# Fused attention and two feed-forward layers: the first weight conversions start ten steps later, and their raw loads move from the Activation queue to the SyncE queue

## The chip, the cores and the metric

The kernel runs on one NeuronCore of a Trainium2 chip. The metric is device microseconds of one execution, as the median of several runs. The engines are named as the profile names them: PE (TensorE), DVE (VectorE), ACT (ScalarE), POOL (GpSimd) and SP (SyncE, which here only issues DMAs). Before the change the median of three runs is 1136.29 us (1132.78 to 1137.8).

## The reference

Three stages follow one another. An attention whose weights below a threshold are set to zero is followed by a feed-forward layer with a squared ReLU and by a second one with the Mish activation:

```python
# q, k, v: (4 batches, 8 heads, 576 rows, 64)
scores = scale * np.matmul(q, k.transpose(0, 1, 3, 2))
thresh = np.max(scores, axis=-1, keepdims=True) - tau
scores = np.where(scores >= thresh, scores, -1000000000.0)
attn = np.exp(scores - max); attn = attn / (sum + 1e-09)
x = (attn @ v) reshaped to 2304 tokens x 512
# first layer, d_ff = 2048
r = np.maximum(x @ w_in, 0.0);  g = s * (r * r) + b;  x = g @ w_out
# second layer, d_ff = 2048
h = x @ w_in2;  g = h * np.tanh(softplus(h));  out = g @ w_out2
```

## The kernel before

**Attention.** Two heads are one pair, so there are 16 pairs, four for each batch of 576 tokens. Each pair is worked in nine row tiles. For every tile `scores` (L338 to L363) has PE make the score tile S in four matmuls, DVE take the row minimum of the negated scores (ns, L342), ACT the exponential (e, L349), DVE the cut (L353) and POOL the normalisation (L363). `weights_t` (L376 to L387) transposes one chunk on PE into T, which ACT copies to te. `products_v` (L403, L406) multiplies by v into pv in two portions, one after the chunk te_6 and one after te_8; the second ends the pair, and `split_x` (L414, L415) casts pv to xh and xl. Transposed chunks run seven tiles behind the scores. There is one buffer for T, so a transposition waits until ACT has copied the one before it.

**Preparing the next pair.** While a pair is scored, `prep_qk` (L294) transposes the next pair's k and then q, ACT casts the transposed tile to its high part (hik and hiq, L278), DVE subtracts to get the low part (lok and loq, L279), and six (k) or four (q) DMAs of 144 KB move halves of these tiles to the partitions where the score matmuls read them (L299, "moves"). The tiles hi and lo have one buffer each, so hiq can only be written when the moves that read hik have landed. All these DMAs are issued on SP, in order. `self.moved` holds the last move that was issued.

**The first layer's weights.** Its weights arrive as 64-bit floats and are converted in 32 units of 512 KB, by `split_w` (L47). For one unit a DMA loads the raw words (wraw, L59), ACT rescales them (L65), DVE puts the single-precision number together in three operations (wa, L67 to L69), ACT casts it to the high part (wp, L72), and DVE (POOL in the first four pairs) subtracts to get the low part (L73). The unit is then stored to DRAM for later batches (L194, on SP). `split_all` runs units as a pipeline: each call of `next(w1)` loads one more unit and takes every unit under way one step further, so a unit is finished by the fifth call after its load. There are four buffers for the raw words and five (`ring`) for finished units.

**The order of the work.** The first four pairs are issued by a loop of their own in `run` (L804 to L808), since the feed-forward layer needs all four pairs of a batch. In that loop `next(w1)` is called at every tenth step from step 42 on. After it the first layer of batch 0 (`moe1`) and the further attention are woven together by a table of costs, and `first` (L814) calls `next(w1)` once for every unit of the layer. The program's instructions are not executed as they are written: a scheduler of the compiler sets the order on each engine, and it moves conversions ahead of where they are written. `keep_in_program_order` and `issue_after` limit it. In that order each engine works strictly one instruction after another, and a DMA that has to wait for its semaphore or its buffer holds up whatever stands behind it on the engine that issues it.

Of the kernel before, what the change touches and what calls it, by code (L numbers as in the profile page):

```python
# [19 lines left out]
class Fused:  # L20
# [26 lines left out]
    def split_w(self, src, hi, lo, pool, tags, kw):  # L47

        nc = self.nc
        i = self.nd
        self.nd += 1
        n = src.shape[1] * src.shape[2] // 2
        raw = pool.tile([P, n, 2], I32, tag=tags[0], name=f"wraw{i}", **kw)
        self.tc.keep_in_program_order(nc.scalar.dma_start(raw.rearrange("p (c f) w -> p c (f w)", c=src.shape[1]), src))  # L59
        low, high = raw[:, :, 0], raw[:, :, 1]  # L60
        hf = high.bitcast(F32)
        yield
        yield
        a = pool.tile([P, n], I32, tag=tags[1], name=f"wa{i}")
        self.tc.keep_in_program_order(nc.scalar.activation(hf, hf, AF.Copy, scale=2.0 ** -112))  # L65
        yield
        nc.vector.tensor_scalar(a, high, 3, None, op0=ALU.logical_shift_left)  # L67
        nc.vector.scalar_tensor_tensor(a, low, 29, a, op0=ALU.logical_shift_right, op1=ALU.bitwise_or)
        nc.vector.scalar_tensor_tensor(a, high, -0x80000000, a, op0=ALU.bitwise_and, op1=ALU.bitwise_or)  # L69
        yield  # L70
        af = a.bitcast(F32).rearrange("p (c f) -> p c f", c=src.shape[1])
        nc.scalar.copy(hi, af)  # L72
        (nc.gpsimd if self.s2p else nc.vector).tensor_tensor(lo, af, hi.bitcast(F32), op=ALU.subtract)  # L73
# [295 lines left out]
    def weights_t(self, pr, ci, run):  # L369
        nc = self.nc  # L370
        T = self.tp.tile([P, 1024], F32, tag="T", name=f"T{pr}_{ci}")
        E4 = self.sets[pr % 2][3]
        o = ci * 128
        for i in range(4):
            with self.tc.issue_after(run) if run and i == 0 else nullcontext():
                nc.tensor.transpose(T[:, i * 128:i * 128 + 128], self.es[pr, i, "pair"][:, o:o + 128], self.ident)  # L376
        if ci != 4:
            h = 0 if ci < 4 else 1

            c0 = 64 + o - 576 * h  # L380
            nc.tensor.transpose(T[:, 512:640], E4[:, c0:c0 + 128], (self.ident, self.swap)[h])  # L381
        else:

            nc.tensor.matmul(T[:, 512:576], E4[:, 0:128], self.ident[:, HALVES[1]], start=True, stop=False)
            nc.tensor.matmul(T[:, 512:576], E4[:, 576:704], self.ident[:, HALVES[0]], start=False, stop=True)
        te = self.at.tile([P, 576], F32, tag="te", name=f"te{pr}_{ci}", bufs=7)
        nc.scalar.copy(te, T[:, :576])  # L387
        return te
# [30 lines left out]
    def attention(self):  # L419
# [18 lines left out]
        for k in range(N + LAG + 2):  # L438
# [33 lines left out]
            if 0 <= j < N:  # L472
                prj, ci = divmod(j, 9)
                todo = prj, ci, self.weights_t(prj, ci, run)
                yield 550
# [299 lines left out]
    def run(self, ctx):  # L775
# [27 lines left out]
        k = 0  # L803
        while 3 not in self.x:  # L804
            next(att)
            k += 1
            if k >= 42 and k % 10 == 2:
                next(w1)  # L808

        pro.close()  # L810
# [33 lines left out]
        while a_on or m_on:  # L844
            if a_on and (not m_on or (a_done - 5000.0) / a_left <= m_done / m_left):
                with tc.high_priority(offset=200):
                    c = next(att, None)
                a_on = c is not None
                a_done += c or 0
            else:  # L850
                c = next(mo, None)
# [11 lines left out]
        nc = tc.nc  # L863
# [73 lines left out]
```

## Time and profile before

| | us |
|---|---|
| median of three runs | 1136.29 (1132.78 to 1137.8) |
| the profiled execution | 1133.57 |
| its span, first to last instruction | 1131.8 |
| PE busy in the span | 1081.1 (96%) |
| DVE busy | 806.3 (71%) |
| ACT busy | 619.0 (55%) |
| POOL busy | 263.4 (23%) |
| PE time in the chain that ended last | 67% of the span |

The median of the runs is 2.7 us above the profiled execution. PE is the engine that is busy nearly all the time; its busy time is that of pipelined matmuls and so does not say that it works at its peak. [...]

### The profile page before, as it was taken

How to read it: one execution, taken by the hardware profiler on the slowest of the kernel's cores; microseconds unless marked ns; L12 is line 12 of the kernel's file. 1: busy time of each engine (PE TensorE's matmuls, PEld its weight loads, DVE VectorE, ACT ScalarE, POOL GpSimd, SP SyncE). 2: the span in 40 equal slices, each digit the busy share in tenths (PEclk: the TensorE clock that was granted, in tenths of full speed). 3: DMA queues.
4: the chain of work that ended last, by engine and by line, in shares of the span. 5: the costliest groups of instructions: out<-in, count | busy, mean ns of one | idle time of the engine just before them, and what ended most of it. 6: DMA issues, size and time to landing. Idle time of an engine off the chain costs nothing.

```text
span 1131.8 us, 21384 instructions
## 1 busy us (share of the span) xinstructions
PE 1081.1 (96%) x7964; PEld 1018.7 (90%) x7964; DVE 806.3 (71%) x1746; ACT 619.0 (55%) x1153; POOL 263.4 (23%) x306
## 2 busy tenths in 40 slices
PE   7887799999999999999999989999999999999998
PEld 6765599898999998888989879999999999999998
DVE  6987799999666677878866666735696368725782
ACT  4655497684576665667747557634363244513351
POOL 4533273351352442325334301100000000000000
PEclk9998899999999999999999999999999999999999
DMA  7366585966847869689864599977998999996683
GB/s 163 80 169 167 172 256 207 300 199 203 246 135 215 249 222 278 214 292 302 310 211 141 190 355 365 361 268 282 351 383 319 343 420 367 348 336 253 263 294 117
DMA packets 141591, 292.70 MB, mean 259 GB/s; under 512 B 52848, under 2 KB 78960, under 8 KB 133168
## 3 DMA queue, kind: packets, MB, share of 16 engines
q1 hardware_dynamic: 123408, 274.26, 70.8%
q10 hardware_dynamic: 18080, 17.07, 5.2%
q8 instruction: 63, 1.03, 0.4%
q14 instruction: 40, 0.33, 0.1%
HBM read 201.85 MB, written 66.58 MB: 237 GB/s over the span
## 4 chain that ended last, share of the span: by engine, by line
PE 67%; DVE 3%; DMA 3%; ACT 2%; issue 1%; POOL 0%; DVEq 0%; ACTq 0%; POOLq 0%
PE o L748 16%; PE y L503 13%; PE h L503 12%; PE qY L614 6%; PE qX L614 4%; PE qV L614 4%; PE S L338 3%; PE pv L406 3%; PE T L376 3%; DMA wso<-chlo 1%; DMA wi<-wsi 1%; PE pv L403 1%; PE T L381 1%; DMA w<-w 1%; ACT e L349 0%
## 5 line engine op out<-in xcount | busy, mean ns | idle before, releaser
L363 POOL TENSOR_SCALAR e<-e,st 128x576 f32<-128x576 f32 x128 | 133.4, 1055 | 229.0 <-DVE st L358 163.9
L748 PE MATMUL o<-wo,hl 128*128 128x256 f32 x1512 | 177.7, 279 | 0.0
L748 PEld LDWEIGHTS o<-wo,hl 128*128 128x128 f32 x1512 | 177.4, 188 | 0.0
L503 PE MATMUL y<-gh,w 128*128 128x288 f32 x768 | 165.0, 300 | 3.4 <-ACT y L548 1.7
L503 PE MATMUL h<-xh,w 128*128 128x288 f32 x768 | 164.7, 299 | 1.6 <-ACT xh L414 0.7
L342 DVE TENSOR_SCALAR_CACHE_REDUCE ns<-S 128x576 f32<-128x576 f32 x144 | 108.0, 752 | 53.6 <-PE S L338 53.2
L349 ACT ACTIVATE e<-ns,st 128x576 f32<-128x576 f32 x128 | 99.1, 776 | 64.4 <-DVE ns L342 62.0
L387 ACT COPY te<-T 128x576 f32<-128x576 f32 x144 | 91.8, 637 | 72.4 <-PE T L381 61.7
L353 DVE SCALAR_TENSOR_TENSOR e<-ns,st,e 128x576 f32<-128x576 f32 x128 | 114.9, 899 | 22.6 <-ACT e L349 21.6
L503 PEld LDWEIGHTS y<-gh,w 128*128 128x128 f32 x768 | 126.7, 189 | 4.5 <-ACT y L548 2.0
L503 PEld LDWEIGHTS h<-xh,w 128*128 128x128 f32 x768 | 125.8, 188 | 2.9 <-ACT xh L414 1.2
L527 POOL TENSOR_TENSOR gl<-rr,gh 128x288 fp32r<-128x288 f32 x96 | 93.6, 989 | 128.8 <-ACT rr L526 128.8
L503 PE MATMUL y<-gl,w 128*128 128x288 f32 x384 | 113.9, 297 | 0.9 <-POOL gl L527 0.9
L503 PE MATMUL h<-xl,w 128*128 128x288 f32 x384 | 113.5, 296 | 0.0
L338 PE MATMUL S<-KH,Q 128*128 128x288 f32 x320 | 97.2, 320 | 11.2 <-DVE lok L279 4.1
L376 PE MATMUL T<-ident,e 128*128 128x128 f32 x576 | 92.5, 283 | 15.3 <-ACT te L387 14.7
L376 PEld LDWEIGHTS T<-ident,e 128*128 128x128 f32 x576 | 68.7, 144 | 33.0 <-issue 18.0
L338 PE MATMUL S<-KL,Q 128*128 128x288 f32 x320 | 91.6, 302 | 0.0
L614 PE MATMUL qY<-yc,wi 128*128 128x384 f32 x432 | 86.6, 337 | 1.3 <-DVE g L637 1.3
L406 PE MATMUL pv<-te,rawv 128*64 128x288 f32 x576 | 86.6, 416 | 0.0
L614 PEld LDWEIGHTS qY<-yc,wi 128*128 128x128 f32 x432 | 75.6, 188 | 1.9 <-DVE g L637 1.9
L338 PEld LDWEIGHTS S<-KH,Q 128*128 128x128 f32 x320 | 62.3, 195 | 16.0 <-DVE ns L342 6.6
(150 smaller groups left out, 2204.4 us busy)
## 6 DMA issues: line engine op xcount, KB each, us to landing
w<-w SPq DMA_DIRECT2D x96, 512.0 KB, 5.1
wo<-wso SPq DMA_DIRECT2D x42, 1024.0 KB, 7.0
wi<-wsi SPq DMA_DIRECT2D x23, 1024.0 KB, 7.8
wi<-wsi SPq DMA_DIRECT2D x25, 768.0 KB, 7.4
w<-wp SPq DMA_DIRECT2D x32, 512.0 KB, 4.8
wsi<-chli SPq DMA_DIRECT2D x24, 512.0 KB, 5.1
wso<-chlo SPq DMA_DIRECT2D x24, 512.0 KB, 7.1
ycd<-yp SPq DMA_DIRECT2D x14, 768.0 KB, 8.1
```

What stands on the lines that cost most here:

```text
L338: self.scored = nc.tensor.matmul(so, Q[:, c0:c0 + 128], kt[:, ks], start=(i == 0), stop=(i == len(terms) - 1)).ins
L342: nc.vector.tensor_scalar(ns.rearrange("p (h n) -> p h n", h=2), sv, -0.125, 3.0e38, op0=ALU.mult, op1=ALU.min, accum_out=nm[:, c1])
L349: nc.scalar.activation(e, ns, AF.Exp, bias=nm[:, c1], scale=-1.0)
L353: nc.vector.scalar_tensor_tensor(e, ns, nthr[:, c1], e, op0=ALU.is_le, op1=ALU.mult, accum_out=sm[:, c1])
L363: nc.gpsimd.tensor_scalar(t, t, rinv[:, j:j + 1], u[:, j:j + 1], op0=ALU.mult, op1=ALU.add)
L376: nc.tensor.transpose(T[:, i * 128:i * 128 + 128], self.es[pr, i, "pair"][:, o:o + 128], self.ident)
L387: nc.scalar.copy(te, T[:, :576])
L406: ins = self.nc.tensor.matmul(*args, **kw).ins
L503: nc.tensor.matmul(acc[:, :n], w[:, wl, c], rhs[c][xl][:, ts], start=(i == 0), stop=(i == 11))
L527: (nc.vector if b == 3 else nc.gpsimd).tensor_tensor(gl[:, ts], r2, gh[:, ts].bitcast(F32), op=ALU.subtract)
L614: self.nc.tensor.matmul(acc, a, b, start=(first and i == 0), stop=(i == n - 1), skip_group_check=True)
L748: nc.tensor.matmul(bank[p][t], hl[:, gl, j, ts], w[:, 2 * (q % 2) + j, wl], start=(old is None and q + j + k == 0), stop=(q + j + k == 6), ...
```

## The change

In the loop over the first four pairs the conversion is called from step 52 on and not from 42, which makes five calls of six. In the same stretch (`self.s2p` is set) the raw loads are issued on SP and must stand behind the last of the moves issued so far; afterwards they are issued on ACT as before.

```diff
         raw = pool.tile([P, n, 2], I32, tag=tags[0], name=f"wraw{i}", **kw)
-        self.tc.keep_in_program_order(nc.scalar.dma_start(raw.rearrange("p (c f) w -> p c (f w)", c=src.shape[1]), src))
+        dst = raw.rearrange("p (c f) w -> p c (f w)", c=src.shape[1])
+        if self.s2p:
+            with self.tc.issue_after(self.moved):
+                nc.sync.dma_start(dst, src)
+        else:
+            self.tc.keep_in_program_order(nc.scalar.dma_start(dst, src))
...
             k += 1
-            if k >= 42 and k % 10 == 2:
+            if k >= 52 and k % 10 == 2:
                 next(w1)
```

Five lines are added ahead of L65, so a line of the kernel before is found five lines further down in the changed one.

On SP, around the moves of the fourth pair's q (Q) and the fifth pair's k (KH, KL; the preparation runs ahead of the scores, and these ahead of the products), the order before was this; no raw load stands there:

```order
L299 DMA Q_125<-hiq_807 64x576
L299 DMA Q_125<-loq_808 64x576
L250 DMA rawk<-in_k_dram 128x8x64
L251 DMA rawk<-in_k_dram 64x2x64
L299 DMA KH_119<-hik_1005 64x576 x2
```

In the changed kernel two raw loads stand behind the moves of q and ahead of the next load of k:

```order
L304 DMA Q_125<-hiq_804 64x576
L304 DMA Q_125<-loq_805 64x576
L62 DMA wraw_876<-in_moe_w_in_dram 128x4x256
L62 DMA wraw_989<-in_moe_w_in_dram 128x4x256
L255 DMA rawk<-in_k_dram 128x8x64
L256 DMA rawk<-in_k_dram 64x2x64
L304 DMA KH_119<-hik_1000 64x576 x2
```

The next two raw loads stand likewise behind the q moves of the following pair and ahead of a load of k. The fifth stands behind those of the pair after that, and there two stores (w) come between the moves of its high and its low part:

```order
L304 DMA Q_125<-hiq_1331 64x576 x2
L199 DMA w_0_0_1_1588<-wp_0_1_988 128x1024
L199 DMA w_0_0_2_1681<-wp_0_2_1117 128x1024
L304 DMA Q_125<-loq_1332 64x576 x2
L62 DMA wraw_1373<-in_moe_w_in_dram 128x4x256
```

In the kernel before, these two stores stood ahead of the load of q, and the raw loads were not on SP.

On ACT, the first raw load before stood among the copies te of the second pair; the next two and the first rescaling stood around the cast hik of the fifth pair, which comes while the second pair's products end:

```order
L387 COPY te_8_876<-T_8_870 128x576 [waits PE_49]
L59 DMA wraw_879<-in_moe_w_in_dram 128x4x256 [waits DMAHW4_49]
L349 ACTIVATE e_1_964<-ns_1_961,st_929 128x576 [waits DVE_49,Pool_49]
L278 CAST hik_1005<-tpk_996 128x640 [waits DMAHW2_49,DMAHW0_49,PE_49]
L349 ACTIVATE e_2_983<-ns_2_980,st_929 128x576 [waits DVE_49,Pool_49]
L65 ACTIVATE wraw_763<-wraw_763 128x512 [waits DMAHW6_49]
L59 DMA wraw_994<-in_moe_w_in_dram 128x4x256 [waits DMAHW7_49]
L414 CAST xh_899<-pv_839 128x576 [waits PE_49]
```

In the changed kernel no instruction of the conversion stands there:

```order
L392 COPY te_8_873<-T_8_867 128x576 [waits PE_49]
L283 CAST hik_1000<-tpk_991 128x640 [waits DMAHW7_49,DMAHW1_49,PE_49]
L354 ACTIVATE e_2_980<-ns_2_977,st_926 128x576 [waits DVE_49,Pool_49]
L419 CAST xh_896<-pv_836 128x576 [waits PE_49]
```

At the end of the fourth pair the order of ACT before, from the last conversion to the copy te_6 and the exponentials behind it:

```order
L72 CAST wp_1_0_1234<-wa_1605 128x512 [waits DVE_49]
L65 ACTIVATE wraw_1607<-wraw_1607 128x512 [waits DMAHW4_49]
L59 DMA wraw_1791<-in_moe_w_out_dram 128x4x256 [waits DMAHW1_49,Activation_49]
L387 COPY te_5_1318<-T_5_1312 128x576 [waits PE_49]
L349 ACTIVATE e_0_1205<-ns_5_1364,st_1196 128x576 [waits DVE_49]
L387 COPY te_6_1357<-T_6_1351 128x576 [waits PE_49]
L349 ACTIVATE e_1_1231<-ns_6_1413,st_1196 128x576 [waits DVE_49]
L349 ACTIVATE e_2_1262<-ns_7_1431,st_1196 128x576 [waits DVE_49]
```

In the changed kernel a cast, three rescalings and three raw loads stand between te_6 and te_7:

```order
L392 COPY te_6_1345<-T_6_1339 128x576 [waits PE_49]
L70 ACTIVATE wraw_1373<-wraw_1373 128x512 [waits DMAHW4_49]
L64 DMA wraw_1688<-in_moe_w_out_dram 128x4x256 [waits DMAHW7_49,Activation_49]
L354 ACTIVATE e_2_1250<-ns_7_1419,st_1188 128x576 [waits DVE_49]
L70 ACTIVATE wraw_1595<-wraw_1595 128x512 [waits DMAHW5_49]
L64 DMA wraw_1779<-in_moe_w_out_dram 128x4x256 [waits DMAHW0_49,Activation_49]
L77 CAST wp_1_0_1363<-wa_1686 128x512 [waits DVE_49]
L70 ACTIVATE wraw_1688<-wraw_1688 128x512 [waits DMAHW7_49]
L64 DMA wraw_1851<-in_moe_w_out_dram 128x4x256 [waits DMAHW1_49,Activation_49]
L392 COPY te_7_1394<-T_7_1388 128x576 [waits PE_49]
L354 ACTIVATE e_3_1297<-ns_8_1453,st_1188 128x576 [waits DVE_49]
L392 COPY te_8_1412<-T_8_1406 128x576 [waits PE_49]
```

When the feed-forward layer starts, both kernels have put the same number of these operations behind them on ACT: five casts wp and seven rescalings stand ahead of the layer's first ReLU in either.

## Rows read from the trace of the kernel before

**Rows 1.** Page, the span in 40 slices: busy tenths of PE.
```profile
PE   7887799999999999999999989999999999999998
```
**Rows 2.** Stretches: us, then busy PE, PEld, DVE, ACT, POOL, PEclk, DMA share, GB/s.
```profile
52.96:79.32 26.36, 21.69 (x154) 17.60 (x155) 21.08 (x63) 15.66 (x25) 12.30 (x13) 0.94 0.56 134
79.32:110.75 31.43, 23.42 (x160) 18.96 (x159) 25.44 (x70) 16.99 (x28) 11.28 (x11) 0.89 0.70 175
110.75:140.17 29.42, 22.26 (x134) 16.37 (x133) 21.42 (x60) 14.57 (x24) 6.54 (x5) 0.83 0.64 187
140.17:171.00 30.83, 30.74 (x238) 28.51 (x239) 29.04 (x59) 28.02 (x64) 21.76 (x20) 1.00 0.85 247
```
**Rows 3.** Timeline of ACT, first of the casts xh: start, us, operation.
```profile
52.96 0.64 ACT L414 CAST xh<-pv 128x576 fp32r<-128x576 f32 x1
```
**Rows 4.** Timeline of PE, 84 to 95 us; in brackets the idle before and its releaser.
```profile
88.83 1.11 PE L376 MATMUL T<-ident,e 128*128 128x128 f32 x4 [4.07 <-ACT te L387]
...
94.34 0.30 PE L338 MATMUL S<-KL,Q 128*128 128x288 f32 x1
```
**Rows 5.** Timeline of ACT, 83 to 90 us.
```profile
83.95 0.78 ACT L349 ACTIVATE E<-ns,st 128x576 f32<-128x576 f32 x1 [0.63 <-DVE ns L342]
87.54 0.69 ACT L278 CAST hiq<-tpq 128x640 fp32r<-128x640 f32 x1 [2.81 <-DMA rawv<-in_v_dram]
```
**Rows 6.** DMA issues, 53 to 60 us: count, KB each, median us from issue to landing.
```profile
KH<-hik SPq DMA_DIRECT2D x4, 144.0 KB, 2.8
```
**Rows 7.** DMA issues, 75 to 83 us.
```profile
wraw<-in_moe_w_in_dram ACTq DMA_DIRECT2D x2, 512.0 KB, 5.2
KH<-hik SPq DMA_DIRECT2D x4, 144.0 KB, 6.7
```
**Rows 8.** Timeline of SP, 74 to 84 us, the last two moves of hik.
```profile
80.30 1.35 SPq L299 DMA_DIRECT2D KH<-hik  x2
```
**Rows 9.** Timeline of PE, 96 to 106 us.
```profile
97.71 2.83 PE L406 MATMUL pv<-te,rawv 128*64 128x288 f32 x21
...
105.34 0.40 PE L338 MATMUL S<-KH,Q 128*128 128x288 f32 x1 [2.24 <-DVE lok L279]
```
**Rows 10.** Timeline of DVE, 102 to 106 us.
```profile
102.59 1.36 DVE L67 TENSOR_SCALAR wa<-wraw 128x512 int32<-128x512 int32 x2 [2.35 <-ACT wraw L65]
...
104.47 0.81 DVE L279 TENSOR_TENSOR lok<-tpk,hik 128x640 fp32r<-128x640 f32 x1
```
**Rows 11.** Timeline of ACT, 118 to 138 us.
```profile
121.03 0.68 ACT L65 ACTIVATE wraw<-wraw 128x512 f32<-128x512 f32 x1
124.32 0.41 ACTq L59 DMA_DIRECT2D wraw<-in_moe_w_out_dram  x1
124.77 0.64 ACT L387 COPY te<-T 128x576 f32<-128x576 f32 x1 [3.07 <-DMA rawq<-in_q_dram]
...
126.83 0.64 ACT L387 COPY te<-T 128x576 f32<-128x576 f32 x1 [0.74 <-PE T L381]
...
133.54 0.64 ACT L387 COPY te<-T 128x576 f32<-128x576 f32 x1 [4.32 <-PE T L381]
```
**Rows 12.** Timeline of PE, 120 to 133 us.
```profile
125.47 1.11 PE L376 MATMUL T<-ident,e 128*128 128x128 f32 x4 [2.82 <-ACT te L387]
...
128.06 4.69 PE L406 MATMUL pv<-te,rawv 128*64 128x288 f32 x21
```
**Rows 13.** DMA issues, 114 to 121 us.
```profile
wraw<-in_moe_w_out_dram ACTq DMA_DIRECT2D x1, 512.0 KB, 7.8
...
rawq<-in_q_dram SPq DMA_DIRECT2D x1, 256.0 KB, 9.2
```
**Rows 14.** DMA issues, 120 to 150 us.
```profile
wraw<-in_moe_w_out_dram ACTq DMA_DIRECT2D x2, 512.0 KB, 4.4
```
**Rows 15.** Timeline of PE, 130 to 143 us: first and last of 18 layer matmuls.
```profile
133.20 0.38 PE L503 MATMUL h<-xh,wp 128*128 128x288 f32 x1
...
135.54 0.30 PE L503 MATMUL h<-xh,wp 128*128 128x288 f32 x1
```

## What the change will do to the time

> **What bounds the kernel now.** The first view is the line of the page that shows PE's busy share in 40 slices [rows 1]: from the sixth slice on PE is at nine tenths or more nearly everywhere, and the first five slices, about 28 us each, are at seven or eight. So what can be won or lost by an edit to the first weights lies in the first 140 us, in which only attention gives PE work. The second view cuts this part at the casts xh, each of which ends a pair; there are four of them, the first at 52.96 us [rows 3] and the last at 140.17, the end of the third stretch [rows 2]. The second pair takes 26.36 us, the third 31.43 and the fourth 29.42. In these stretches PE has 21.7 to 23.4 us of busy time and a granted clock of 0.94, 0.89 and 0.83, while behind them, from 140.17 to 171.00, it is busy 30.74 of 30.83 us at a clock of 1.00. Once the fourth pair is done, PE has the feed-forward layer to fill every gap. A microsecond by which the fourth xh comes earlier is therefore a microsecond of the whole time, as long as nothing behind it becomes late.
>
> The third view is the timeline of PE there, for what it waits on. Three waits matter. At 88.83 a transposition starts after 4.07 us of idle time, because ACT had not copied the tile before it [rows 4]. ACT had stood still for 2.81 us ahead of the cast hiq [rows 5], which stands before that copy in its order. The profile names a DMA as the releaser, and hiq writes a tile that four moves KH still read. The last two of these were issued by 81.65 (80.30 + 1.35) [rows 8], and in this stretch such a move took 6.7 us to land, beside two raw loads of 512 KB [rows 7]: 88.3, which is about where hiq starts. Twenty us earlier, with no raw load near, the same moves landed in 2.8 us [rows 6]. The second wait is 2.24 us at 105.34 for lok [rows 9]; DVE had put three operations of the conversion before it, from 102.59 to 104.47 [rows 10]. The third is 2.82 us at 125.47 [rows 12], again for a copy: ACT idled 3.07 us before it, since a raw load in its order could only be issued at 124.32 [rows 11]. It waited for a semaphore that the load of q had taken at 115.0; that load took 9.2 us to land, among stores, moves and a raw load of 7.8 us [rows 13].
>
> **The change part by part.** The profiled execution is 1133.57 us, and the terms are set against it.
>
> T1, the third pair. The two raw loads that ran beside these moves now stand behind the moves of the q before, more than 9 us earlier, and the rescaling and the DVE work of unit 0 leave this pair until its end. If the moves land in 2.8 us again, they are there at 84.45 (81.65 + 2.8), and hiq can start when ACT has ended E, at 84.73 (83.95 + 0.78). That is 2.81 us sooner than 87.54. PE's wait shrinks from 4.07 to 1.26. After the wait PE ran at its lower level until 94.34, where the 128x288 matmul is back at 0.30 us [rows 4]: 5.5 us at half rate, which cost 2.7. A wait of 1.26 may or may not lower the clock; I take half of the 2.7. T1 is 2.8 + 1.3 = 4.1 us gained. Its bounds are 0, if something else holds hiq, and 6.8, if the whole wait and the whole slow stretch go.
>
> T2, lok. Before it DVE now has one shift and one combination of unit 0, not two shifts and a combination. Of the 1.88 us [rows 10] one operation of 0.68 goes. I take 0.7 gained, between 0 and 2.24.
>
> T3, the raw load that held ACT. In the changed order the load of q is issued ahead of two of the stores that stood before it, no raw load is in flight beside it, and the first load that ACT issues itself comes after te_4 and waits for a small part of q. I take the 2.82 us as gone. The products behind it ran at the lower clock: 21 matmuls in 4.69 us [rows 12] where 2.83 is usual [rows 9]. I take half of these 1.9 as well, so T3 is 3.7 us gained. Its bounds are 0 and 4.7.
>
> T4, what is paid. Between te_6 and te_7 ACT now has three rescalings of 0.68, a cast wp of about the same length and three issues of 0.41, 3.95 us, and an exponential [rows 11]. Before, nothing of the conversion stood there, and te_7 came 6.7 us after te_6 (133.54 against 126.83), waiting for PE. PE's cover behind its part of te_6 is 18 layer matmuls (133.20 to 135.54 and 0.30: 2.6 us [rows 15]), the first products (2.83), one transposition and two score tiles (about 0.6 to 0.9 each): 7.5 us. The third of the rescalings needs the raw load issued right after the first; at the quiet landing time of 4.4 us [rows 14] te_7 starts about 0.64 + 0.68 + 0.41 + 4.4 + 0.68 + 0.41 = 7.2 us after te_6 and ends at 7.9. That alone is 0.4 us more than the cover. In addition the first rescaling may find its own data late, since the fifth raw load is issued behind the last moves of q, and the cast wp waits for three DVE operations. I charge 2.0 us. The bounds are 0 and 6.8, two landings of 7.8 in place of 4.4 [rows 13, 14].
>
> Behind the fourth pair nothing is left to be done that was done before: the same five casts and seven rescalings are behind both kernels when the layer starts, and each later unit keeps its place relative to the ring of five. One subtraction goes from POOL to DVE, 0.7 us on an engine that is then at 29.04 of 30.83 [rows 2]; beside a full PE I cost it at nothing.
>
> The sum is 4.1 + 0.7 + 3.7 - 2.0 = 6.5 us gained, 1127.1 for an execution like the profiled one. The median of the runs before lies 2.7 above that one, so I forecast 1130 us.
>
> [...]
>
> **The rivals.** A, the tail takes most of it back. T1 to T3 come as forecast (8.5), but both raw loads in the tail land in 7.8 us and T4 is 6.8: 1136.3 - 1.7 = 1134.6. For it: ACT works in order, and te_7 stands behind all three rescalings. Against it: the loads and stores that crowded the stretch from 114 to 121 us are partly gone by then.
>
> B, the raw loads were not what held hiq and lok; moves of k collide with the load of k anyway. Then T1 and T2 are 0, T3 is half, 1.9, T4 stays 2.0, and the time is that of before, 1136. For it: even the second pair has a wait of this kind in its 26.36 us, and its clock is 0.94. Against it: 2.8 us against 6.7 for the same moves.
>
> C, slower. ACT becomes the bound of the fourth pair's end. Each of the three raw loads of the tail lands in 7.8 us and each waits for the one before to be issued: 3 x 3.4 = 10.2 us more, and PE, idle for so long, falls to its lower clock and loses 2.7 as it did after the 4.07. That is T4 = 14.9 with the 2.0, against gains of 8.5 at best: 1142.7. It decides as soon as te_7 comes more than about 16 us after te_6 (the 7.5 of cover and the 8.5 gained). For it: such a DMA on ACT did wait 3.07 us in the kernel before. Against it: it needs all three to be late together.
>
> **How the numbers follow.** The forecast gets 0.48, A 0.22, B 0.16, C 0.14. A difference of 0.5%, 5.7 us, is about the least that a measurement of this kernel can tell from no change. Faster than 1130.6 are two thirds of the forecast's own cases, and with them a part of those in which T1 and T3 come near their upper bounds and the tail costs nothing: 0.44. Slower than 1142.0 are C and a little of B: 0.15, since the order of the matmuls changes up to 300 us and small waits may appear anywhere. The rest, 0.41, is no change that can be told. With every gain at its upper bound (6.8 + 2.2 + 4.7) and no price the time would be 1122.6, with no gain and T4 at 6.8 it would be 1143.1; the range leaves a tenth at each side, 1124 to 1140.
>
> **What would show it right or wrong.** In the profile after, the stretch between the second and the third xh should fall to about 27 us, with the KH moves of that stretch landing in about 3 us and no wait near 4 us ahead of hiq. No idle time of ACT should be put down to the load of q. The time from te_6 to te_7 of the fourth pair should be 8 to 10 us, with PE idle for 1 to 3. The forecast is wrong if the third stretch stays over 30 us (then B), if te_7 comes 12 us or more after te_6 (A, or C beyond 16), or if PE shows new waits on weights after the fourth pair.

## The result, and the profile after

| | before | changed |
|---|---|---|
| median, run side by side | 1136.12 us (1132.78 to 1137.8, 5 runs) | 1124.95 us (1122.47 to 1127.63, 5 runs) |
| the profiled execution | 1133.57 | 1124.95 |
| its span | 1131.8 | 1123.2 |
| fourth xh starts at | 140.17 | 137.00 |
| eighth xh starts at | 317.13 | 310.19 |

The changed kernel takes 0.991 of the time, interval 0.9883 to 0.9937. In a second measurement it took 0.993 (0.9904 to 0.9957).

The stretches between the casts xh answer to [rows 2]. The three lines are the stretch to the second, third and fourth xh; columns as there:

```profile
54.12:80.67 26.55, 21.58 (x153) 17.48 (x154) 21.48 (x64) 15.19 (x24) 12.92 (x13) 0.94 0.58 144
80.67:106.12 25.45, 21.84 (x161) 17.09 (x161) 21.72 (x64) 15.68 (x26) 9.43 (x10) 1.00 0.66 166
106.12:137.00 30.88, 22.59 (x135) 17.29 (x135) 25.38 (x70) 16.47 (x28) 7.76 (x6) 0.83 0.69 209
```

The third pair takes 6.0 us less (31.43 to 25.45), and its granted clock is 1.00, not 0.89 [rows 2]. The fourth takes 1.5 us more (29.42 to 30.88). The first xh comes 1.2 us later than in [rows 3]; in a second execution of the same kernel it came at 52.95, as before the change.

**The third pair.** On ACT, the cast hiq now follows directly behind E, where 2.81 us of idle time stood [rows 5]:

```profile
84.57 0.78 ACT L354 ACTIVATE E<-ns,st 128x576 f32<-128x576 f32 x1
85.25 0.68 ACT L283 CAST hiq<-tpq 128x640 fp32r<-128x640 f32 x1
```

The moves of hik, issued between 77 and 85 us, land in 3.1 us, not 6.7 [rows 7]:

```profile
KH<-hik SPq DMA_DIRECT2D x4, 144.0 KB, 3.1
```

On PE the wait of 4.07 us [rows 4] is gone. The longest ones that are left in this pair are these, the second of them in place of the 2.24 of [rows 9]:

```profile
91.53 0.37 PE L343 MATMUL S<-KH,Q 128*128 128x288 f32 x1 [0.86 <-DMA Q<-loq]
...
101.23 0.40 PE L343 MATMUL S<-KH,Q 128*128 128x288 f32 x1 [1.65 <-DVE lok L284]
```

**The fourth pair, first half.** The load of q, issued between 105 and 114 us, lands in 3.5 us, not 9.2 [rows 13], and ACT issues its first raw load without the wait of [rows 11]; its row has no bracket:

```profile
rawq<-in_q_dram SPq DMA_DIRECT2D x1, 256.0 KB, 3.5
```
```profile
115.22 0.41 ACTq L64 DMA_DIRECT2D wraw<-in_moe_w_in_dram  x1
```

On PE the wait of 2.82 us [rows 12] is gone, and the products behind it take 2.83 us at a granted clock of 1.00, where they took 4.69 at 0.60 (128.06 to 132.75):

```profile
120.90 2.83 PE L411 MATMUL pv<-te,rawv 128*64 128x288 f32 x21
```

**The fourth pair, its end.** ACT from te_6 on (first row) to te_7 (last row):

```profile
119.10 0.63 ACT L392 COPY te<-T 128x576 f32<-128x576 f32 x1
125.00 0.65 ACT L70 ACTIVATE wraw<-wraw 128x512 f32<-128x512 f32 x1 [5.27 <-DMA wraw<-in_moe_w_in_dram]
...
128.75 0.62 ACT L77 CAST wp<-wa 128x512 fp32r<-128x512 f32 x1 [1.88 <-DVE wa L74]
...
129.83 0.62 ACT L392 COPY te<-T 128x576 f32<-128x576 f32 x1
```

The first rescaling waits 5.27 us for the fifth raw load, and te_7 comes 10.7 us after te_6. But it is not te_7 that PE waits for. DVE stands still behind the same rescaling, though the score tile is done at 124.51 (124.22 + 0.29), and only afterwards makes its minimum ns:

```profile
125.68 0.43 DVE L72 TENSOR_SCALAR wa<-wraw 128x512 int32<-128x512 int32 x1 [4.52 <-ACT wraw L70]
...
129.23 0.75 DVE L347 TENSOR_SCALAR_CACHE_REDUCE ns<-S 128x576 f32<-128x576 f32 x1
```

PE waits 5.10 us for that ns. Behind the wait, from 130.05 to 134.04, the granted clock is 0.50, and over the products that follow 0.64: 13 matmuls take 2.91 us, which took 1.86 at 1.00 in the kernel before (last line).

```profile
130.05 0.61 PE L343 MATMUL S<-KH,Q 128*128 128x288 f32 x1 [5.10 <-DVE ns L347]
...
134.04 2.91 PE L411 MATMUL pv<-te,rawv 128*64 128x288 f32 x13
```
```profile
138.26 1.86 PE L406 MATMUL pv<-te,rawv 128*64 128x288 f32 x13
```

What the late load met is read from the DMA issues of 109 to 120 us (count, KB each, median us to landing). SP issued its own in the order Q<-hiq, two stores w, Q<-loq, raw load; ACT issued the raw load of 115.22 beside them:

```profile
w<-wp SPq DMA_DIRECT2D x3, 512.0 KB, 5.1
wraw<-in_moe_w_in_dram ACTq DMA_DIRECT2D x1, 512.0 KB, 7.9
wraw<-in_moe_w_in_dram SPq DMA_DIRECT2D x1, 512.0 KB, 7.1
Q<-hiq SPq DMA_DIRECT2D x2, 144.0 KB, 2.5
Q<-loq SPq DMA_DIRECT2D x2, 144.0 KB, 7.1
```

Of two equal moves, the one ahead of the stores landed in 2.5 us and the one behind them in 7.1; so did the raw load. But both of the late ones also ran beside ACT's raw load, which took 7.9 us itself. This trace alone doesn't tell the stores ahead from the load beside; e2 and e4 below bear on it. The three raw loads that ACT issues later, from 125.06 to 129.19, were not late:

```profile
wraw<-in_moe_w_out_dram ACTq DMA_DIRECT2D x3, 512.0 KB, 4.3
```

**Behind the fourth pair.** From the fourth to the eighth xh the kernel before took 176.96 us and the changed one takes 173.19. The prediction had nothing there. The granted clock is 1.00 over this stretch in both. PE's waits from the fifth to the eighth xh, in the kernel before (179.10 to 317.13: total, times, longest):

```profile
PE S L338 <- DVE lok L279: 1.0, 1, 1.0
PE tpq L270 <- DVE ns L342: 0.9, 1, 0.9
PE y L503 <- DVE y L550: 0.5, 1, 0.5
PE y L503 <- ACT r L524: 0.4, 1, 0.4
PE pv L403 <- ACT te L387: 0.2, 1, 0.2
```

and in the changed kernel (174.38 to 310.19):

```profile
PE S L343 <- DVE loq L284: 0.4, 1, 0.4
PE pv L408 <- ACT te L392: 0.2, 1, 0.2
```

The edit touches no instruction there. What differs is the order in which the scheduler gives PE attention and layer. Counted in that order, before the change 180, 408 and 624 matmuls of the layer are issued by the end of the fifth, sixth and seventh pair (order A), in the changed kernel 168, 372 and 600 (order B). By the end of the eighth it is 786 in both. So in order B attention stands a little earlier among the layer's matmuls. In the changed kernel this begins with one more score tile ahead of the last products of the fourth pair. From the fourth to the eighth xh both kernels have the same 768 matmuls of the layer, and the changed one has 148 score matmuls where the kernel before has 152. So one score tile, about 0.6 us at a granted clock of 1.00 (123.74 to 124.35 in the changed kernel), is in the 3.8 us won there but was moved and not saved.

### The profile page after: what moved, and what is told of

Same layout as the page of the kernel before. It is cut to its first block, busy times and chain, and to the rows that moved or that the text cites. A ratio compares the mean times of both kernels' runs of the same rounds, so it can differ in the third digit from the quotient of the medians.

```text
span 1123.2 us, 21390 instructions
## 1 busy us (share of the span) xinstructions
PE 1077.8 (96%) x7964; PEld 1016.8 (91%) x7964; DVE 802.3 (71%) x1747; ACT 617.6 (55%) x1153; POOL 263.6 (23%) x305
## 4 chain that ended last, share of the span: by engine, by line
PE 74%; DVE 5%; DMA 5%; ACT 3%; issue 2%; POOL 1%; SPq 0%; ACTq 0%; DVEq 0%; POOLq 0%
PE o L753 16%; PE y L508 16%; PE h L508 13%; PE qY L619 6%; PE S L343 5%; PE qX L619 4%; PE qV L619 4%; PE pv L411 4%; PE T L381 3%; DMA wi<-wsi 1%; PE pv L408 1%; DMA wso<-chlo 1%; PE T L386 1%; ACT e L354 1%; DMA wraw<-in_moe_w_in_dram 1%
## 5 line engine op out<-in xcount | busy, mean ns | idle before, releaser
L368 POOL TENSOR_SCALAR e<-e,st 128x576 f32<-128x576 f32 x128 | 137.2, 1085 | 227.2 <-DVE st L363 182.5
```

The costliest lines, as they stand in the source:

```text
L368: nc.gpsimd.tensor_scalar(t, t, rinv[:, j:j + 1], u[:, j:j + 1], op0=ALU.mult, op1=ALU.add)
```

## The experiments

Ratios are against the kernel before, measured on the same chip, with their interval; the stretches are read from one profiled execution each. "3rd" and "4th" are the stretches that end with that xh. That execution need not be a typical one: that of e5 took 1118.40 us, the least of its six, and that of e9 1129.37, the most of its six.

| kernel | calls from | raw loads | order | 3rd | 4th | 4th xh at | 5th to 8th xh | ratio |
|---|---|---|---|---|---|---|---|---|
| before | 42 | ACT | A | 31.43 | 29.42 | 140.17 | 138.03 | 1 |
| changed | 52 | SP, behind | B | 25.45 | 30.88 | 137.00 | 135.81 | 0.991 (0.9883 to 0.9937) |
| e7, the same again | 52 | SP, behind | B | 25.13 | 30.82 | 135.68 | 135.79 | 0.993 (0.9904 to 0.9957) |
| e1 | 52 | ACT | A | 29.50 | 26.04 | 133.80 | 138.04 | 0.9974 (0.9955 to 0.9994) |
| e2 | 42 | SP, behind | B | 28.38 | 26.29 | 135.62 | 135.81 | 0.9924 (0.99 to 0.9948) |
| e6 | 52 | SP, anywhere | A | 25.14 | 28.73 | 139.28 | 137.92 | 0.9999 (0.9977 to 1.0022) |
| e3 | 52 | SP, one call ahead | A | 25.71 | 25.14 | 131.25 | 137.98 | 0.9904 (0.9883 to 0.9924) |
| e4 | 53 | SP, behind | A | 26.65 | 26.00 | 132.67 | 138.60 | 0.9944 (0.9924 to 0.9964) |
| e5 | 58 | SP, one call ahead | B | 24.13 | 27.86 | 131.67 | 135.67 | 0.99 (0.9877 to 0.9923) |
| e8 | 44 | ACT | B | 24.51 | 29.91 | 134.60 | 135.66 | 0.9923 (0.9893 to 0.9953) |
| e9 | 48 | SP, one call ahead | B | 32.35 | 26.95 | 138.18 | 135.80 | 0.9912 (0.9878 to 0.9947) |

**e1, the later start alone.** In the kernel before:

```diff
-            if k >= 42 and k % 10 == 2:
+            if k >= 52 and k % 10 == 2:
```

> The later start alone: the conversion is called from step 52 on, five times, and its raw loads stay on ACT's queue. The order still has two of these loads around the cast hik of the fifth pair, beside the moves KH. Theory (the raw loads beside the moves are what cost): the KH moves there still land in about 6 us, the stretch from the second to the third xh stays at 29 to 31 us (31.43 before, 25.45 with the whole change), and the time is 1131 to 1135. Rival (what pays is that ACT and DVE have less conversion to do in that stretch): the stretch falls to about 26 us and the time to about 1126.

Measured: 1129.36 us, 1.6 less than the theory's least. The third stretch falls only to 29.50, as the theory had it; raw loads on ACT still run beside the moves, which take 4.7 us here. ACT waits for the moves by name:

```profile
86.36 0.69 ACT L278 CAST hiq<-tpq 128x640 fp32r<-128x640 f32 x1 [3.59 <-DMA KH<-hik]
```

The fourth stretch is 26.04: T3's wait is gone, and in the tail PE waits for no more than 0.70 us. A wait of 2.99 us for a copy te at 117.27, further ahead, is left.

**e2, the queue alone.** In the changed kernel:

```diff
-            if k >= 52 and k % 10 == 2:
+            if k >= 42 and k % 10 == 2:
```

> The queue alone: raw loads on SP behind the moves, but the conversion called six times from step 42 on. Theory: the KH moves land in about 3 us although unit 0 is converted beside them, the stretch between the second and third xh falls to 27 or 28 us, and the time is 1126 to 1130. Rival (the later start pays): the stretch stays at 30 us or more and the time near 1134.

Measured: 1125.13 us. The moves land in 3.2 us, but hiq still waits for them a little:

```profile
86.25 0.69 ACT L283 CAST hiq<-tpq 128x640 fp32r<-128x640 f32 x1 [1.31 <-DMA KH<-hik]
```

The third stretch, 28.38, and the time lie just outside what was expected. At the end of the fourth pair a raw load on SP is late here too. It stands behind the moves of q with no store between, but beside a raw load of ACT, and ACT waits 4.17 us for it:

```profile
wraw<-in_moe_w_out_dram ACTq DMA_DIRECT2D x1, 512.0 KB, 6.4
wraw<-in_moe_w_in_dram SPq DMA_DIRECT2D x1, 512.0 KB, 6.8
```
```profile
124.02 0.66 ACT L70 ACTIVATE wraw<-wraw 128x512 f32<-128x512 f32 x1 [4.17 <-DMA wraw<-in_moe_w_in_dram]
```

PE loses only 1.53 us to it, in a wait for the copy te that follows.

From the first to the fourth xh each part alone wins more (5.8 us in e1 and 5.9 in e2) than both together (4.3, and 4.5 in e7): only with both does PE wait 5 us for what stands behind the late load. But e2 ends with the changed kernel's time and e1 does not. In the profiled executions e1 is 1.8 us ahead of e2 at the fourth xh and 1.6 behind at the eighth; between the two e2 has order B. Another 3.8 us lie behind the eighth xh and are not explained by it.

**e6, the common queue without the order in it.** In the changed kernel:

```diff
-            with self.tc.issue_after(self.moved):
-                nc.sync.dma_start(dst, src)
+            nc.sync.dma_start(dst, src)
```

> The whole change, but nothing holds the raw loads behind the moves: the scheduler puts four of them at the very start of SP's order, behind the first pair's moves and ahead of the second pair's loads and moves, and the fifth ahead of the q moves of the last of these pairs. If a common queue is served in order, the second pair's moves wait for 2 MB of raw words, about 5 us, and the first xh comes 4 to 6 us later than at 54.12; the end of the fourth pair loses its wait of 5.10 us for the fifth load, so the time is 1123 to 1128. If order in the queue does not matter, the first xh stays at 54 and the time falls to about 1119.

Measured: 1132.68 us, no gain; the time expected was missed. Four raw loads now stand at the start of SP ahead of the second pair's moves, and the first xh comes at 61.05. ACT waits for these moves with the cast hiq, and PE for loq, which is made from it:

```profile
30.93 0.69 ACT L282 CAST hiq<-tpq 128x640 fp32r<-128x640 f32 x1 [7.88 <-DMA KH<-hik]
```
```profile
32.53 0.61 PE L342 MATMUL S<-KH,Q 128*128 128x288 f32 x1 [7.00 <-DVE loq L283]
```

Up to the first xh the place behind the moves is worth 6.9 to 8.1 us (against 54.12 and 52.95). The third stretch is short here too (25.14). That no gain is left is not all due to the missing order in the queue, since this run has order A as well.

**e3, each raw load one call ahead.** `split_w` takes a load that was issued before; there are five raw buffers:

```diff
+                if k < 92:
+                    ...
+                    self.ahead[self.nd] = self.raw_load(self.nd, src, self.pre, ("raw", "ra"), dict(bufs=5))
```

> The whole change, with each raw load of the first four pairs issued one call earlier than its unit is started (five buffers for raw words in place of four). All five loads then stand behind the q moves of the two earlier pairs, and on ACT no rescaling but one stands between te_6 and te_7. Theory (the wait of PE of 5.10 us at 124.95 in the changed kernel is the fifth raw load, which lands 7.1 us after its issue behind two stores): the wait goes, and with it the lower clock behind it; from the third to the fourth xh it takes about 25 us in place of 30.88, and the time is 1117 to 1121. Rival (another wait takes its place, for ACT or DVE have the same work to do there): 28 us or more, and 1122 to 1126.

Measured: 1122.52 us; 1117 to 1121 was missed. The theory on the wait holds: the 5.10 is gone and the fourth stretch takes 25.14 us, not 30.88. But of the 5.75 us that the fourth xh comes earlier than in the changed kernel, only 2.1 are left at the eighth (308.11 against 310.19). This is the run that asked for another cause: e3 has order A.

**e4, every call one step later: order A with the loads on SP.** In the changed kernel:

```diff
-            if k >= 52 and k % 10 == 2:
+            if k >= 53 and k % 10 == 3:
```

> The changed kernel once more, so that the next two kernels are compared with it on one chip. Up to the fourth xh 137 us (132 us without the wait for the fifth raw load), from the fourth to the eighth xh 173.2 us; 0.990 to 0.993 of the kernel before.

> The changed kernel with every conversion call one step later (53, 63, ... 93). The raw loads stay on SP behind the moves, five calls stay five, and the fifth load stays late; but the scheduler's order on PE from the fourth xh on is that of the kernel before (180 and 408 layer matmuls issued ahead of the fifth and sixth pair's end, the changed kernel has 168 and 372). Theory O (the 3.6 us that the changed kernel wins between the fourth and the eighth xh come from the order in which attention and layer are woven, not from the loads): that stretch takes 176.9 us as in the kernel before, against 173.2, and the whole is 3 to 4 us slower than the changed kernel, about 0.994 to 0.995 of the kernel before. Rival (they come from the loads on SP, for instance fewer waits on ACT in the layer): the stretch takes 173.2 us and the time is that of the changed kernel within 1 us.

Measured: e7 1124.37 us; e4 1126.17 us, so 1.8 us slower than e7 and not the 3 to 4 expected; the intervals of the two ratios overlap. The stretch from the fourth to the eighth xh took 178.4 against 173.1 us in e7. PE in the last three of its four parts, sum of e4:

```profile
sum 138.60, PE 135.07 PEld 125.70 DVE 119.88 ACT 89.15 POOL 51.80; mean PE 45.02 PEld 41.90 DVE 39.96 ACT 29.72 POOL 17.27
```

One part of the expectation was wrong, and instructive: the fifth load was not late. Here SP issued it behind the moves of q alone, without stores between, and ACT issued no raw load until 119.64, when it had landed. It took 4.0 us, and the fourth stretch is 26.00, which gave back part of what order A cost. Beside e2 (6.8 us with no store ahead) this says that no store need stand ahead of it to make it late. The load beside is the likely reason, though in e2 two stores were issued right behind it too.

```profile
wraw<-in_moe_w_in_dram SPq DMA_DIRECT2D x1, 512.0 KB, 4.0
...
Q<-loq SPq DMA_DIRECT2D x2, 144.0 KB, 2.4
```

**e5, loads ahead and order B.** In e3:

```diff
-            if k >= 52 and k % 10 == 2:
+            if k >= 58 and k % 10 == 8:
```

> The kernel whose raw loads are issued one call ahead (1122.5 us), with its calls at steps 58, 68, 78, 88, so four conversions instead of five ahead of the layer. The order on PE behind the fourth xh then is nearly that of the changed kernel (168, 372 and 600 layer matmuls at the ends of the fifth to seventh pair). Theory O: the fourth xh at 131 to 132 us as with the loads ahead, 173.2 to 174 us from there to the eighth xh instead of 176.9, in all 3 to 4 us less than 1122.5: 1118 to 1120, 0.987 of the kernel before. Rival: 176.9 us and 1122.5. A third possibility is that with one conversion fewer the layer waits for its weights (a wait of PE on L426's successor units, 1 to 3 us), which would hide the gain.

Measured: 1121.85 us (1118.4 to 1124.47). From the fourth to the eighth xh it takes 173.00 us, as theory O said, and the eighth xh comes at 304.67, the earliest of all. The median is 2 to 4 us above the expectation; behind the fourth xh PE waits 1.91 us once, for the cast xh and not, as the third possibility had it, for weights. Its ratio is the lowest here, but its interval overlaps with that of e7 on the same chip, so that it beats the changed kernel is not settled.

**e8, order B with the raw loads on ACT.** In the kernel before:

```diff
-            if k >= 42 and k % 10 == 2:
+            if k >= 44 and k % 10 == 4:
```

> The kernel before with its six conversion calls two steps later (44, 54, ... 94), raw loads on ACT as before. The scheduler's order on PE behind the fourth xh then is that of the changed kernel (168, 372, 600 layer matmuls at the ends of pairs five to seven). Theory O (order alone): 135.7 us from the fifth to the eighth xh, as in every kernel with this order, against 138.0 in the kernel before; up to the fourth xh nothing of the changed kernel's gain, within 2 us of 140; in all 0.996 to 0.998 of the kernel before. Rival (the loads on SP make the stretch short): 138.0 us and no change in time.

Measured: 1124.85 us, a larger gain than expected; the fourth xh comes at 134.60, where 138 to 142 was expected. The stretch behind the fifth xh is as theory O has it; here is its sum, and below it that of the kernel before:

```profile
sum 135.66, PE 135.17 PEld 126.52 DVE 116.21 ACT 88.22 POOL 52.66; mean PE 45.06 PEld 42.17 DVE 38.74 ACT 29.41 POOL 17.55
```
```profile
sum 138.03, PE 135.09 PEld 125.71 DVE 120.05 ACT 89.19 POOL 51.85; mean PE 45.03 PEld 41.90 DVE 40.02 ACT 29.73 POOL 17.28
```

PE is busy equally long, with 12 matmuls of the layer more and one score tile fewer in order B; the idle time falls from 2.9 to 0.5 us. DVE is busy 3.8 us less. So the order on the other engines changes with that on PE, and no run tells which of them removes the waits. What was not expected: two steps were enough to take the raw loads away from the moves of the third pair, on ACT's own queue. The moves issued between 74 and 88 us landed in 3.2 us, and hiq started without a wait:

```profile
KH<-hik SPq DMA_DIRECT2D x4, 144.0 KB, 3.2
```
```profile
84.60 0.68 ACT L278 CAST hiq<-tpq 128x640 fp32r<-128x640 f32 x1
```

One pair later the raw loads meet the moves, which land in 6.0 us beside three of them, and the old wait is back, which is in the fourth stretch of 29.91:

```profile
113.42 0.69 ACT L278 CAST hiq<-tpq 128x640 fp32r<-128x640 f32 x1 [2.40 <-DMA KH<-hik]
```

**e9, loads ahead, one call earlier than e5.** In e5:

```diff
-            if k >= 58 and k % 10 == 8:
+            if k >= 48 and k % 10 == 8:
```

> The kernel with the loads one call ahead and calls at 58 to 88, here from step 48 on, so five conversions ahead of the layer as in the changed kernel, in the changed kernel's order on PE. If the 1.9 us that PE waits behind the fourth xh there come from conversions that fall into the layer, they go and the time is 1119 to 1121 us, 0.988 of the kernel before; if not, it is that of the kernel with calls from 58 on (1121.85, 0.990), or 1 us more because the earlier raw loads stand beside more moves.

Measured: 1123.93 us; 1119 to 1121 was missed. The wait of 1.91 us behind the fourth xh is gone (the longest from there to the fifth is 0.2), but the time is not gained. The conversions now lie in the third pair, which takes 32.35 us. After a wait of 1.78 us for ns the products take 5.09 us instead of 2.83, and the granted clock over the pair is 0.84:

```profile
95.56 5.09 PE L418 MATMUL pv<-te,rawv 128*64 128x288 f32 x21
```

## Why the prediction came out as it did

The profiled span fell by 8.6 us; forecast for it were 6.5, and the median fell by 11.2 (8.7 in e7). The direction and the mechanisms of the first four pairs were right. T1 to T3 together won 2.2 us more than forecast, T4 cost 4.1 more, and a gain behind the fourth pair was not seen at all.

T1 and T2 were right in mechanism. Forecast were 4.1 and 0.7 in the third stretch, 4.8 together; measured are 6.0. hiq starts at the end of E and the granted clock is 1.00 for the whole pair. The half rate that T1 counts with is in the trace of before: from 88.83 to 94.34 the granted clock was 0.51. lok gave 0.6, so T1 is 5.4, between the 4.1 taken and its bound of 6.8. That raw loads beside the moves are the cause, against rival B, is shown twice: by the changed kernel, where the moves land in 3.1 us, and by e8, where they land in 3.2 us without the common queue. The queue is thus one way to do it, the time of the call another. e1 and e2 add that the later start alone leaves 29.50 us for the third stretch and the queue alone 28.38.

T3 was right, at its upper bound: the 2.82 us went, and the products took 2.83 us, not 4.69, so 4.7 against 3.7. Behind both waits I had counted half of the slow clock as won; none of it is left (1.00 in the third pair and in these products).

T4 had the right place and the wrong size. The fourth stretch grew by 1.5 us although T3 took 4.7 away, so the tail cost 6.1 by difference (in it the score tile that moved there), near the upper bound of 6.8, where I charged 2.0. The failed step is the sentence "the first rescaling may find its own data late": I named it and priced it as a remainder. It was the main term, 5.27 us of idle time on ACT. PE met it first through the ns that DVE could not make, for which the cover of 7.5 us that I worked out for te_7 did not count. te_7 was late by the same rescaling: with ns in time, PE would have done the score tile by about 125.6 and then waited for te_7, copied at 130.45 (129.83 + 0.62). That is an estimate from these rows, and it makes the second wait nearly as long as the first. e3 shows that the late load is the cause: with the loads one call ahead the fourth stretch takes 25.14 us.

In SP's order the late load stood behind two stores. That this order is what made it late the traces don't show: the raw load took 7.1 us behind two stores and beside a raw load of ACT (changed kernel), 6.8 with no store between, a load beside and two stores behind it (e2), and 4.0 with none of these (e4). What each adds is not separated.

Rival A came near with its price (6.8), but not by its way: the raw loads that ACT issues in the tail landed in 4.3 us, as I had forecast with 4.4, and the late one was on SP. Its time did not come, because T1 and T3 came out above the forecast and because of the next point. Of my own signs, te_7 at 8 to 10 us after te_6 was just missed (10.7) and the 1 to 3 us of idle PE were missed (5.1). C did not come: none of its three loads was late.

Up to the fourth xh this is 6.0 - 1.5 = 4.5 us won, less 1.2 for the late first xh and 0.2 in the second pair: 3.2. Forecast were 6.5.

The rest was missing. The failed step is "Behind the fourth pair nothing is left to be done that was done before". True of the work, but not of its order: the scheduler chose order B, and the way from the fourth to the eighth xh became 3.8 us shorter. It takes 173.00 to 173.52 us in the six executions in order B and 176.81 to 178.44 in the five in order A. All six executions in order B take 135.66 to 135.81 us from the fifth to the eighth xh, and all five in order A 137.92 to 138.60, whether the raw loads are on ACT (before, e1, e8) or on SP (the others). So it goes with the order and not with the loads; e8 and e4 are the two made to separate them. I had counted the changed order only as a risk. That the time is inside the range is in part due to two misses of opposite sign, T4's 4.1 too little and the order's 3.8 not seen; so far it was luck. The median, 1124.95, is 1 us from the lower end of the range.

The last 1.7 us, behind the eighth xh, I can't assign: from there to the end the eleven profiled executions take 811.9 to 817.7 us, those in order A 813.1 to 817.7 and those in order B 811.9 to 816.3, with no run that tells them apart. The work of PE there is the same before and after (5890 matmuls in either trace), and 1.4 of the 1.7 us are idle time of PE. The spread among the eleven goes in part with the granted clock of single executions: behind the eighth xh it is 1.00 in every 40-us stretch of the first 800 us in e2, e3 and e5 (811.9 to 813.1), and 0.92 to 0.96 in one or two of them in each of the others, at different places in the changed kernel and in e7, which are the same kernel. Why the scheduler takes order B in some kernels is open as well: with the loads on ACT it takes A for calls from 42 and B for 44, with the loads on SP it takes B for 52 and A for 53.

## What to carry to other kernels

When a transfer is moved to another queue, price it by what it then stands behind and by what runs beside it on the other queue, and follow each engine that works in order behind its consumer, not just the one that comes first to mind: one late load left ACT idle for 5.27 us here and DVE for 4.52. Where a scheduler sets the order, an edit in one stage can reorder the next one; count its order on the bound engine there before writing "nothing changes": here the other order went with 3.8 us less behind the fourth xh, though the longest wait that is gone between the fifth and the eighth was 1.0 us, and 3.2 us were won up to the fourth. Two transfers can be taken apart by time as well as by queue: two steps gave here in the third pair what the whole change gave there (24.51 us against 25.45).

## What the runs showed of the hardware

Beside two 512-KB raw loads the 144-KB moves took 6.7 us [rows 7] and 4.7 (e1), without them 3.1 (changed kernel) and 3.2 (e2, e8). Equal moves on SP took 2.5 us ahead of two 512-KB stores, and 7.1 behind them and beside a 512-KB load on ACT's queue (changed kernel). A 512-KB load on SP took 7.1 us behind stores and beside a load (changed kernel), 6.8 beside a load with two stores issued behind it (e2), and 4.0 with none of these (e4). After the wait of 5.10 us in the changed kernel the granted clock of PE was 0.50 from 130.05 to 136.00 us and 1.00 from 136.50 on; after the 0.86 and 1.65 us of its third pair it was 1.00. After a wait of 1.78 us in e9 the same score matmul took 0.61 us, as at 0.50 in the changed kernel (130.05). The longer wait was not always the one with the slower matmuls: in e8 the score matmul behind a wait of 0.83 us took 0.61 us, and the one ahead of it, behind a wait of 2.11, took 0.40, as at 1.00 in the changed kernel (101.23):

```profile
113.37 0.40 PE L338 MATMUL S<-KH,Q 128*128 128x288 f32 x1 [2.11 <-DVE ns L342]
...
115.03 0.61 PE L338 MATMUL S<-KH,Q 128*128 128x288 f32 x1 [0.83 <-DVE loq L279]
```
